# First q block on ScalarE's DMA queue, ahead of the activation table, with a new order of jobs

## The chip, the cores and the metric

The kernel runs on one core of a Trainium2 chip. Five engines work side by side: TensorE (PE in the profile; its weight loads are PEld), VectorE (DVE), ScalarE (ACT), GpSimd (POOL) and SyncE (SP), which here only issues DMAs. Each engine takes its own instructions in program order and waits on semaphores for the others. The metric is the device time of one execution in microseconds (us).

## The reference

Three layers in float32 (weights arrive as float64 bits):

1. Attention for q, k, v of shape 2 x 8 x 768 x 64. Each query sees the keys less than 16 positions away and, for each of 24 blocks of 32 keys, one summary: the maximum of the block's keys (score plus log 32) with the mean of its values. Softmax runs over both kinds of score at once.
2. A gated layer on x (2 x 768 x 512): `h = relu(x @ w_in)`, split into u and v; v is normalised per row, multiplied from the left by `w_spatial` (768 x 768), `b_spatial` is added, and `(u * v) @ w_out` is returned.
3. A convolution layer: `h = relu(x @ w_in)`, a three-tap convolution along the sequence, `(h * sigmoid(conv)) @ w_out`.

## The kernel before

Eight head pairs (2 batches x 4 pairs, n = 0 to 7) are worked on, each in two **groups** of six blocks of 64 queries, so 16 groups. A group is (`group`, line 447): scores on TensorE (`qk`: mask rows at L462 and L469, then 24 small matmuls of q against the scaled keys at L475); the negated row maximum on VectorE (L479); six exponentials with running sums on ScalarE (L483, twelve instructions); sum and reciprocal on VectorE (L486, L489); the scaling of the probabilities on GpSimd or VectorE (L492); two steps of three transposes on TensorE (L496), each copied out of PSUM (L518); 24 matmuls with the values (L502); and the split of the result in a high and a low part (L523, L524). The scores have two PSUM buffers, so group i + 2 waits until the exponentials of group i are done.

Before the groups of a pair, `keys` (line 379) scales the key windows (two halves, L388 or L390), takes block maxima over k (L398, two halves for the first four pairs) and places them scaled beside the windows (L404). `means` (line 409) makes the block means of the values: for pairs 0 and 2 with matmuls (L418), for the others with a reduction and a transpose (L425, L428), then copies them into place (L430, L437).

The weights arrive as float64 bits. `convert` (line 288) loads a part, builds the float32 with one product (L294 or L295) and three VectorE instructions (L297, L299, L301), and splits it in a high part (L285) and a low part (L279). Every dense product is then three matmuls (`mm3`, L310 to L312). The dense work of batch 0 is put between the attention steps of the later pairs as soon as its inputs exist; behind the attention only dense work is left.

What the engines do and in which order is set by two strings. Each piece of work is a job that is added with `add` (a dictionary of the engines that may do it with a cost in us, then what it reads and writes). `PICK` chooses the engine where there is a choice, and `ORDER`, two characters to a job, is the order in which the jobs are emitted, and so the program order on every engine and queue. `Plan.order` also keeps a clock of its own from the costs (jobs of the DMA queue are called "Q", and what they load counts as there `LAND` = 2.6 us after their cost). It uses that clock for one thing only: where a TensorE job ahead of the dense work would start at least 0.5 us after the previous one, it emits (gap - 0.1) / 0.22 filling matmuls on a constant tile (`warm`, L741). Seven warming matmuls of the same line start the program.

All DMAs are issued by SP's queue, in the order k (two parts), a part of w_in, the first half of q, k of the second pair, and so on. On ScalarE the first instruction is a dummy exponential (L736), which brings the load of the activation table with it.

Of the kernel before, what the change touches and what calls it, by code (L numbers as in the profile page):

```python
# [41 lines left out]
RATE = 276.0  # L42
# [13 lines left out]
    "EtDpEuC7C8C9C+C-BXEiDqDBCLFiEvFjE3E4EjEkDzD0EwFvCMCNDuDvCOCPD6DCDDDED7D8D9D1D+D2EEEFD3FBCQEGE5EmDFDGFkEHEIE6D4F6F7EOEPEQ"
    "ERGmD5F8F9C4FCD-EAEBECFWEXE7FFFGEYEZEaEbGnFHFIFJFKElFXEDE8GlEcEdE9FYFLGkFZFlFaGQGRGDE+ExEJEKELESHRGSGEGFEyFmE-FAFnEzFbFz"
    "F0EMFwGtG6GdEVJ8FQFRFcFdF1ENHHHIGeF2F3GfGGGgF4FeHSFSFTF5FoHJFUHTGhGiGjFpFqFrGuFDG7HUHVHKHLEWFsG8GTGUGHF+GVGIFtHMHNFuFfFg"
    "HlHmFxHnHoGJFyG9G+HOHWHbHcGvGKGwHdHXFhHpHYItGLGMF-GxGyGAHZH5GBHqIDH6HeGWGXIyGCH7FEGoH8HPHfHgGYHrHvGNGZGaGbHwHxHaGOGcGPHh"
    "G-H9H+HQGzG0HyGpGqLNIEG1G2GsGrH-IFIuHAHzH0HBIzINIOIPHCIIIvHsIAHiH1H2HtHuHDH3H4IBICIXIiI0HEG3IJIKHFLOLPHGILISI1G4G5HjI2Hk"  # L60
    "ITInIdIaIUIQIYIZIMLQIjIqJ5IVIWIkIlIGIRIoIpI6LRIHIbIcI3JHJIJJImIrIeJbLbI9I+JKIwJvI7IsJLJMI8JNJwI4I-JAIfJBJCJDJcI5JRJSIgJT"
    "JUJVJWJXJOJPJdJeJfJYJgJhJQJiIxKRJxJyKbJzJ0KHKIKJKKKLKlJjKmKMJkKNIhJEJFKSLULWJGKvJ9JlJmJnJoJpJqKwLDLEK5KOLSLTKPKQLVKcJ1Li"
    "J2JrJsK6KTK7J+J-LXKdKeLYJ3JtLdJ4KxLZKAKfKgJZLaLcLpKhJuKiKnKBKCKULFKVKjJaKkLeLGLHLfLkLgLhLjLwKDKyKzKWKXKYK0K1KZKEKFMrK8K9"
# [728 lines left out]

# [101 lines left out]
```

## Time and profile before

| | |
|---|---|
| runs before | 333.34 us median of 3 (331.83, 333.34, 337.34) |
| profiled execution | span 329.8 us from first to last instruction; its time with what lies around the span is not listed |
| busy, share of the span | PE 98%, PEld 82%, DVE 71%, ACT 57%, POOL 21% |
| granted TensorE clock, mean | 0.999 |
| DMA | 34.50 MB, mean 105 GB/s |

How to read it: a busy TensorE is not yet a useful one, since the filling matmuls count as busy. What an engine waits for stands behind "idle before" with the releaser. The chain of waits goes back from the last instruction, at each step to what released it. What matters for the start of the kernel lies in the first 40 us; all engines but GpSimd are close to full there, one after the other.

### The profile page before, as it was taken

How to read it: one execution, taken by the hardware profiler on the slowest of the kernel's cores; microseconds unless marked ns; L12 is line 12 of the kernel's file. 1: busy time of each engine (PE TensorE's matmuls, PEld its weight loads, DVE VectorE, ACT ScalarE, POOL GpSimd, SP SyncE). 2: the span in 40 equal slices, each digit the busy share in tenths (PEclk: the TensorE clock that was granted, in tenths of full speed). 3: DMA queues.
4: the chain of work that ended last, by engine and by line, in shares of the span. 5: the costliest groups of instructions: out<-in, count | busy, mean ns of one | idle time of the engine just before them, and what ended most of it. 6: DMA issues, size and time to landing. Idle time of an engine off the chain costs nothing.

```text
span 329.8 us, 6175 instructions
## 1 busy us (share of the span) xinstructions
PE 324.2 (98%) x2388; PEld 269.1 (82%) x2388; DVE 232.8 (71%) x435; ACT 189.6 (57%) x466; POOL 67.9 (21%) x86
## 2 busy tenths in 40 slices
PE   8999999999999999999999999999999999999996
PEld 3768888888888888888988888888888888888886
DVE  6989799877766456788989788689988776470000
ACT  3999889977357323534425355788857665461111
POOL 4695835641230131211001011200000000000000
PEclk9999999999999999999999999999999999999999
DMA  7999486905026600232334234400000010000101
GB/s 221 344 284 322 116 276 223 267 21 145 0 72 194 219 0 0 80 112 72 122 127 127 70 123 127 129 0 2 0 2 32 0 66 32 32 32 34 64 32 66
DMA packets 13325, 34.50 MB, mean 105 GB/s; under 512 B 1648, under 2 KB 3952, under 8 KB 13296
## 3 DMA queue, kind: packets, MB, share of 16 engines
q1 hardware_dynamic: 13296, 34.11, 33.5%
q8 instruction: 19, 0.31, 0.4%
q14 instruction: 10, 0.08, 0.1%
HBM read 30.96 MB, written 3.15 MB: 103 GB/s over the span
## 4 chain that ended last, share of the span: by engine, by line
PE 93%; ACT 2%; POOL 1%; DMA 1%; issue 0%; DVE 0%; SPq 0%; ACTq 0%; POOLq 0%
PE late L311 12%; PE late L310 12%; PE late L312 12%; PE mm L310 10%; PE mm L311 9%; PE mm L312 9%; PE pt L496 3%; PE xp L311 3%; PE xp L312 3%; PE xp L310 3%; PE pt L311 3%; PE xp L502 3%; PE pt L312 3%; PE pt L310 3%; PE s L475 2%; DMA a<-q_in 1%
## 5 line engine op out<-in xcount | busy, mean ns | idle before, releaser
L689 DVE SCALAR_TENSOR_TENSOR v<-v,conv_t 128x767 f32<-128x767 f32 x32 | 32.4, 1016 | 12.2 <-ACT v L686 11.8
L483 ACT ACTIVATE a<-s,a 128x120 f32<-128x120 f32 x96 | 33.4, 385 | 1.0 <-DVE a L479 0.9
L294 ACT ACTIVATE a<-a 128x512 f32<-128x512 f32 (+1 forms) x28 | 17.8, 636 | 16.4 <-DVE w L279 7.7
L299 DVE SCALAR_TENSOR_TENSOR a<-a,a 128x512 uint32<-128x512 uint32 (+1 forms) x32 | 19.9, 623 | 3.5 <-ACT a L294 1.7
L483 ACT ACTIVATION_READ_ACCUMULATOR a<-s,a 128x1 f32 x96 | 22.1, 231 | 0.0
L492 POOL TENSOR_TENSOR a<-a,a 128x720 f32<-128x720 f32 x14 | 19.7, 1419 | 5.5 <-DVE a L489 5.4
L301 DVE SCALAR_TENSOR_TENSOR a<-a,a 128x512 uint32<-128x512 uint32 (+1 forms) x32 | 20.0, 624 | 0.9
L310 PE MATMUL late<-xh,a 128*128 128x512 f32 x48 | 18.7, 389 | 0.0
L311 PE MATMUL late<-xl,a 128*128 128x512 f32 x48 | 18.7, 389 | 0.0
L312 PE MATMUL late<-xh,a 128*128 128x512 f32 x48 | 18.7, 389 | 0.0
L279 POOL TENSOR_TENSOR w<-a,w 128x256 fp32r<-128x256 f32 (+1 forms) x11 | 10.6, 969 | 38.8 <-ACT w L285 38.7
L692 ACT ACTIVATE v<-v 128x768 f32<-128x768 f32 x16 | 13.5, 843 | 8.4 <-DVE v L689 8.4
L570 POOL TENSOR_TENSOR stat<-stat,mhalf 128x1 f32<-128x1 f32 x12 | 9.1, 762 | 43.4 <-DVE stat L567 39.8
L496 PE MATMUL pt<-ident,a 128*120 128x128 f32 x96 | 16.5, 280 | 0.8 <-DVE a L518 0.6
L730 ACT COPY tmp<-late 128x512 f32<-128x512 f32 x7 | 4.1, 585 | 21.9 <-PE late L312 21.9
L695 DVE TENSOR_TENSOR v<-v 128x768 f32<-128x768 f32 x15 | 14.3, 954 | 3.1 <-ACT v L692 2.9
L565 DVE BATCH_NORM_STATS2 stat<-tmp 128x6 f32<-128x512 f32 x12 | 8.3, 691 | 11.4 <-ACT tmp L562 11.3
L285 ACT CAST w<-a 128x512 fp32r<-128x512 f32 (+1 forms) x15 | 8.3, 550 | 13.9 <-DVE a L301 13.9
L686 ACT ACTIVATE v<-v,conv_t 128x768 f32<-128x768 f32 x16 | 15.0, 938 | 1.8 <-DVE w L279 1.0
L496 PEld LDWEIGHTS pt<-ident,a 128*120 128x120 f32 x96 | 10.8, 137 | 5.3 <-POOL a L492 1.0
L518 ACT COPY a<-pt 120x384 f32<-120x384 f32 x21 | 10.3, 488 | 8.1 <-PE pt L496 7.9
L479 DVE TENSOR_REDUCE a<-s 128x6 f32<-128x720 f32 x16 | 14.2, 899 | 1.0 <-PE s L475 0.8
(336 smaller groups left out, 1033.0 us busy)
## 6 DMA issues: line engine op xcount, KB each, us to landing
a<-w_in SPq DMA_DIRECT2D x12, 512.0 KB, 3.6
a<-w_out SPq DMA_DIRECT2D x8, 512.0 KB, 3.6
out<-tmp SPq DMA_DIRECT2D x11, 256.0 KB, 2.0
a<-vwin SPq DMA_DIRECT2D x8, 288.0 KB, 6.1
a<-v_in SPq DMA_DIRECT2D x6, 384.0 KB, 6.0
a<-vwin SPq DMA_DIRECT2D x4, 576.0 KB, 5.9
tmp<-w_spT SPq DMA_DIRECT2D x6, 384.0 KB, 3.5
a<-w_in SPq DMA_DIRECT2D x8, 256.0 KB, 6.4
```

The costliest lines, as they stand in the source:

```text
L294: mul = {"ACT": (0.2 + n / 1080, lambda: ACT.mul(fu.f(), half(1).bitcast(F32), 2.0 ** -112)), "POOL": (0.18 + n / 1050, lambda: POOL.tenso ...
L299: add({"DVE": (0.16 + n / 960, lambda: DVE.scalar_tensor_tensor(out=last.u(), in0=fu.u(), scalar=0x80000000, in1=last.u(), op0=ALU.bitwise ...
L301: add({"DVE": (0.16 + n / 960, lambda: DVE.scalar_tensor_tensor(out=fu.u(), in0=fu.u(), scalar=3, in1=last.u(), op0=ALU.logical_shift_left ...
L310: PE.matmul(ps, lhsT=lh, rhs=rh, start=first and i == 0, stop=False)
L311: PE.matmul(ps, lhsT=lh, rhs=rl, start=False, stop=False)
L312: PE.matmul(ps, lhsT=ll, rhs=rh, start=False, stop=last and i == n - 1)
L483: ACT.activation(out=e[:, u, :NK], in_=sv[:, u // GA, u % GA], func=AF.Exp, bias=st[:, 0, u:u + 1], accum_out=sm[:, u, :1])
L492: eng.tensor_tensor(out=e, in0=e, in1=st[:, 1].unsqueeze(2).to_broadcast([128, GB, NK]), op=ALU.mult)
L496: PE.transpose(pt3[:NK, a], e[:, GA * h + a, :NK], ident)
L686: add({"ACT": (0.93, lambda: ACT.activation(out=ct.f(), in_=hh.f(), func=AF.Copy, scale=conv_t[:, 3 * f + 1:3 * f + 2]))}, r + 0.5, [hh.to ...
L689: DVE.scalar_tensor_tensor(out=ct.f()[:, to], in0=hh.f()[:, of], scalar=conv_t[:, 3 * f + k:3 * f + k + 1], in1=ct.f()[:, to], op0=ALU.mul ...
L695: eng.tensor_tensor(out=ct.f(), in0=hh.f(), in1=ct.f(), op=ALU.mult)
```

## The change

The load of the first half of q of the first head pair becomes a job of its own kind, "QA": `ACT.dma_start`, with a cost of 2.0 us in the planner. It is the first job of the new order. The dummy exponential becomes a job too (`table`) and comes fourth, so that on ScalarE the DMA issue stands ahead of the load of the activation table. The other loads stay on SP. Some planner costs change (the very first w_in part counts 165 KB more; the casts of `one_tile` count 0.6 us, with the table counted apart). `ORDER` and `PICK` are new from end to end.

```diff
 ORDER = (
-    "AAACABADAFAgAEAiAGAjAZAaAkAhAbAHAqAcAdAeArALBYAfAMBZBbBaBcAIA3A4AsAJAlAtASAUATAVAWAuAvANBiBjAKBEA5A6A7BFCTCRCUBkAmAnAwAx"
+    "AIABAGAAAHADACAFAiAaAjAkAlAEAcAMAhANAJAbBbBZArAsAOAdA4ATBcAeAKA5BdBaBFAPAUAtBjAmBGALAfB9AuAvAVAWBkA6AwCUAxA7BHA8BIAyBwB+"
...
-                t = max(t, end[j][0] + (self.LAND if end[j][1] == "Q" else 0.0 if end[j][1] == e else self.HAND))
+                t = max(t, end[j][0] + (self.LAND if end[j][1] in ("Q", "QA") else 0.0 if end[j][1] == e else self.HAND))
...
-        dma(0.8 * n, lambda: SP.dma_start(raw.u(), src.bitcast(U32)), rank - lead, writes=[raw.tok()])
+        dma(0.8 * n + (165 if rank - lead < 3 else 0), lambda: SP.dma_start(raw.u(), src.bitcast(U32)), rank - lead, writes=[raw.tok()])
...
-            dma((q1 - q0) / 2 * 0.84 + (166 if n + i == 0 else 0), lambda q0=q0, q1=q1: SP.dma_start(qts[j].ap[:, q0:q1], q_in[b, p][:, q0:q1]), r - 9 + 1.5 * i, writes=[qts[j].tok(q0, q1)])
+            on = {"Q": ((q1 - q0) / 2 * 0.84 / RATE, lambda q0=q0, q1=q1: SP.dma_start(qts[j].ap[:, q0:q1], q_in[b, p][:, q0:q1]))}
+            if n + i == 0:
+                on = {"QA": (2.0, lambda q0=q0, q1=q1: ACT.dma_start(qts[j].ap[:, q0:q1], q_in[b, p][:, q0:q1]))}
+            add(on, r - 9 + 1.5 * i - (100 if n + i == 0 else 0), writes=[qts[j].tok(q0, q1)])
...
-    ACT.activation(out=stat[0][:, 11:12], in_=mhalf, func=AF.Exp)
...
+    def table():
+        ACT.activation(out=stat[0][:, 11:12], in_=mhalf, func=AF.Exp)
+
+    add({"ACT": (2.2, table)}, -100, writes=[tok("table")])
...
-    add({"ACT": (2.65, one_tile)}, -99, [tok("ident")], [mask_b.tok(sub="o")])
+    add({"ACT": (0.6, one_tile)}, -99, [tok("ident"), tok("table")], [mask_b.tok(sub="o")])
```

The two strings, read two characters at a time and split by engine, begin like this (g0, g1 are a pair's two halves; w1b and w1a the second and first half of the first w_in tile; numbers of pairs and groups count from 0):

```
SP queue   before  k0a k0b w1b q0a | k1a k1b q0b vals0a w1a q1a vals0b k2a k2b q1b
           after   k0a k0b w1b     | k1a k1b q0b q1a w1a vals0a k2a q1b k2b vals0b     (q0a on ScalarE)
ScalarE    before  table casts scale(0,g1) w1b-high exp0 w1a-product exp1 scale(2,g0) exp2 mean copy w1a-high exp3 exp4 copy split copy exp5
           after   q0a table casts scale(0,g0) w1b-product scale(1,g1) exp0 exp1 exp2 copy scale(2,g1) exp3 copy split exp4 split copy scale(3,g1) exp5
VectorE    before  ... scale(0,g0) masks max k0a, k0b, place | w1b shift, or, or | max scores0 | max k1b, k1a | max scores1 | sum0 w1a x3 recip0
           after   ... masks max k0a, k0b, place | w1b shift | max k1a | max scores0 | w1b or | max k1b | w1b or | max scores1 | sum0 recip0
GpSimd     before  constants w1b-product scale(1,g0) w1b-low scale(1,g1) place1 normalise0 normalise1
           after   constants scale(0,g1) scale(1,g0) place1 w1a-product w1b-high normalise0 scale(2,g0) normalise1
TensorE    before  qk0 qk1 m0a qk2 m0b t0 qk3 t0 qk4 t1 pv0 t1 t2 qk5 pv1 t2 qk6 t3 m1 t3 dense qk7 pv2
           after   qk0 qk1 qk2 m0a t0 qk3 t0 m0b t1 qk4 t1 pv0 qk5 t2 pv1 qk6 t2 m1 m2a t3 qk7 pv2 dense
```

Here qk is the scores of a group, t one of its two transpose steps, pv its value product, m a pair's block-mean step. The planner's rule for filling matmuls, followed with each string and its costs, gives 6, 5 and 4 of them before (ahead of qk0, qk1 and the first t2) and 2, 3, 6 and 2 after (ahead of qk0, qk1, qk2 and qk6); the seven warming ones stay. In the whole string 88 jobs change their engine (GpSimd has 76 jobs before and 98 after, VectorE 391 and 375, ScalarE 286 and 281). The number of TensorE jobs stays at 515; its changes of tiling mode fall from 45 to 42. The last eight jobs of SP's queue stay as they are.

## Rows read from the trace of the kernel before

**Rows 1.** The page's first part: busy us (share of the span) and instructions of each engine.

```profile
PE 324.2 (98%) x2388; PEld 269.1 (82%) x2388; DVE 232.8 (71%) x435; ACT 189.6 (57%) x466; POOL 67.9 (21%) x86
```

**Rows 2.** Windows: stretch, its us, busy us of each engine, clock, DMA share, GB/s.

```profile
0.00:6.00 6.00, 4.96 (x21) 1.80 (x21) 3.27 (x25) 2.54 (x5) 1.97 (x12) 1.00 0.60 173
6.00:40.00 34.00, 32.53 (x591) 24.90 (x585) 29.85 (x70) 30.08 (x133) 26.37 (x33) 1.00 0.91 280
40.00:320.00 280.00, 280.00 (x1741) 236.06 (x1737) 199.71 (x343) 155.63 (x326) 39.53 (x42) 1.00 0.27 84
2.00:4.00 2.00, 2.00 (x7) 0.62 (x5) 0.98 (x8) 0.82 (x4) 0.60 (x3) 1.00 0.87 254
```

**Rows 3.** Windows of line L741 alone (PE and PEld busy, clock, DMA share, GB/s).

```profile
0.00:6.00 6.00, 4.87 (x13) 1.66 (x13) 1.00 0.60 173
6.00:40.00 34.00, 2.28 (x9) 0.80 (x9) 1.00 0.91 280
```

**Rows 4.** The chain of waits in order of time, 0 to 40 us: start, us, what.

```profile
2.08 4.27 DMA a<-q_in
6.49 0.88 PE s L475 x24
7.39 0.92 DVE a L479
8.33 2.17 ACT a L483 x12
...
24.67 0.12 PE mm L310
25.93 0.85 PE xp L502 x24
27.25 2.73 PE mm L418 x24
29.98 0.47 PE pt L496 x3
```

**Rows 5.** Timeline, 0 to 25 us: start, us, engine, line, operation [idle before <-releaser].

```profile
0.71 1.28 ACT L736 ACT_TABLE_LOAD   x1 [0.71 <-PEq L887]
0.72 0.85 SPq L363 DMA_DIRECT2D a<-k_in  x2
1.04 4.87 PE L741 MATMUL mm<-ones 128*128 128x512 bf16 x13 [1.04 <-DVE mhalf L735]
2.01 0.20 ACT L736 ACTIVATE stat<-mhalf 128x1 f32<-128x1 f32 x1
2.08 0.43 SPq L366 DMA_DIRECT2D a<-q_in  x1
2.12 0.49 ACT L767 CAST a<-ident 64x64 bf16<-64x64 f32 x2
3.21 0.46 DVE L390 TENSOR_SCALAR a<-a 128x576 f32<-128x576 f32 x1 [0.91 <-DMA a<-k_in]
3.76 0.68 ACT L388 ACTIVATE a<-a 128x576 f32<-128x576 f32 x1 [1.15 <-DMA a<-k_in]
4.39 0.54 DVE L398 TENSOR_REDUCE a<-a 128x12 f32<-128x384 f32 x1
4.97 0.31 DVE L404 TENSOR_SCALAR a<-a 128x288 f32<-128x288 f32 x1
5.76 0.29 DVE L297 TENSOR_SCALAR a<-a 128x256 uint32<-128x256 uint32 x1 [0.48 <-DMA a<-w_in]
6.97 0.81 POOL L390 TENSOR_SCALAR a<-a 128x576 f32<-128x576 f32 x1 [0.64 <-DMA a<-k_in]
8.21 1.00 DVE L398 TENSOR_REDUCE a<-a 128x12 f32<-128x384 f32 x2
24.13 0.54 PE L496 MATMUL pt<-ident,a 128*120 128x128 f32 x3 [0.61 <-DVE a L518]
```

**Rows 6.** Windows of all engines, from the first exponentials to the end of the sixth set.

```profile
8.30:24.60 16.30, 15.24 (x295) 11.45 (x295) 14.31 (x34) 15.70 (x80) 13.48 (x17) 1.00 1.01 315
```

More of the change, by code (lines that the diff above doesn't have):

```diff
@@ L56 @@
[L56 to L63, printed above, removed]
@@ L72 @@
-    "S0S1SZS2SsS3S4StS7S5SuS8S6TuS9SvS+SwTIS-TJTBTKTCTLTMTDTNTETOTPTFTSTQT7TTTGTRTUTHTVTfTWTgTYThTZTiTjTaTkTbTlTmTcTpTnTqTdTo"
-    "TrTeTsT2TtT3TvT4TwT5UDTxT6UET8UFTyT9UGUHTzUIT+T0UJT1UKT-UNULUAUOUMUPUBUQUCURUSUTUUUXUVUYUWUZUaUbUcUdUeUhUfUiUgUjUkUlUmUn"
-    "UoUrUpUsUqUtUuUvUwUxUyU1UzU2U0U3U4U5U6U7U8U-U9VAVBU+VCVDVEVFVGVJVHVKVIVLVMVNVOVPVQVRVS"
+    "AIABAGAAAHADACAFAiAaAjAkAlAEAcAMAhANAJAbBbBZArAsAOAdA4ATBcAeAKA5BdBaBFAPAUAtBjAmBGALAfB9AuAvAVAWBkA6AwCUAxA7BHA8BIAyBwB+"
+    "BLCSBlA9CVAzAnBxCWA0AXBmBnAoAQA+A-B-CTDICcByApBoDKBAA1DLAqCpARCdCEBBA2BzA3BpBNB0BeBJAYBMCqCeDMBCBDCAC2AZBOBEBqDSDJB1CFBr"
@@ new lines @@
+    "CfCgBsBfBKC3BgCrCXBPDTB2DfBiBhEfCsCtB3ASCuBtDxEUB4ChEhCYDUCLBuDgBSDVDWC4B5EiCiBvCZCjBQDhB6CGCkCHCIB7ClCaEgEoB8AgCvDiCwDX"
+    "CbCBCmFPEpCnCxCyBRCJE1CoDjDNEqCKBUDYCDEVCzDZBTFQC0C1DyErDsFNDaC6DODPDzDkEsDbDtCCJ6DlEjE2DRDQFCDcDdDeDmEtFODnC7C8DoDuC9EW"
+    "C+E3EuFwDpCMBVFWDqFjC-DBDADrBWEvBXFDDvCND0DwCOBYJ9D1EkEwE4E5D2D7FkEYF7DCD3FXE6D4CPD5DDFlElD8D6FGD9F8D+DEEADFExCQE7CREZD-"
+    "FRDGEBF9C5FYEFEGEaE8DHEHECE9GmFHEIEnEbEcEDFEF+EEF0FxGnFZE+FaFyEmGEGRFIGeGoGFEyFbGSEJFJE-EdFKEeEKFmGGELFLEPEQFAFnEzF1EREM"
@@ new lines @@
+    "ESFBENF2FMGlGTFcETGuEOF3GfG7HSHIE0F4GgFdFFGhFSF5FeF6GiHTFoEXGjHJHUFfHKGkFpG8HLFTGHFUGUFqHMHVFrHWFsGIFVF-HcGJFgHNFtGvFuFv"
+    "HmHdGwGKHOHPGLHnGpHoG9FzGMGVFhHeHfIuHgHpFiGWGNIjGXGAHXGYHqHQGxHwGBH6G+GZHxHYGCH7GyGDIkHZIEGaHaHrGbGOG-GzIzGPGcH8HyGdGQHz"
+    "G0HAIFHRIGG1HbH0G2H9HhI0IOG3GqH1HBIvH+GrHsHCHtIJGtH-H2LOGsIPIAHDHiH3IBIKG4HEHFIlG5HGH4IQG6ILHHLQIRHjH5I1I2HuITIMIULVIHIm"
+    "ICIIHvHkISIVIWIDIYIeIXI+INIfIZJIJJIwHlLPJSIoIgIaJcIbIpIhI-JdI3LRInJTJKJUIcIqIdJeIiJwIrIsJ7JLI4ItJVJMLSJmJAI7I5JNI6JnJWJx"
@@ new lines @@
+    "JBJXLcI8IxJOI9JCJfIyKIJPJDJgJyKmJEJhJQJzJoJiJRKcKdJ+J-JYJ8JFJZJpJGJHKAJ0J1KwKSKxJqLEJaKeK6K7KJJrLTLFKnLGLUJbJjLHLWKTJsLX"
+    "KBJ2KKK8KCJ3KLLYKMLZKDJ4KUJ5JkLaLbKfLjLeJtKNKyKgKEJlKoKFLdKpLfKOKVKPKhLgKWLILhLlKiLJJuKQLiKzKjNAMsLqK0LkK1LmLnKRKGK9K2Mt"
+    "JvMuKkK3LoKHKXKYKlLxLKNBKqK+LsM2KZKrKaLpK-MvK4MiLrM3MwKbLANeLtLuLBNfNoLLK5LvM4LwNULzLCLMNpLyMjNCM5L0KsNVKtNDL1L4NgLNNhNW"
+    "MkLDMxM6NiL2L3NKNEMlL6NLMmMyL5M7NXKuKvL-MnL7NFL8L9M8M9O2NqNGMoNMO3L+NNNjM+O8MzNOMBNYMAO4MCO9MDMENHMFMGMIM0NIMHMNMpNrMUM-"
@@ new lines @@
+    "MqNsO5NPMJMKO+MPOqNZMLMMO-MONkMQMROwOrM1MWOsMrO6MbMSOxNtMTOtNaNQPOPCNlMVPAPIMXOyMYOuNJNRPPPDO7NyMZNuPJMaOvMdPaNbPEMcOzPU"
+    "MePBO0PxPKMfN0MgPQPVMhO1PyPbNmPLPRNzPSPsPFN1NSN2NvN5PfPTN3PGOANnPcPdQQPMQRN7PeNTPzPgN4PhPHP0NcN6P2N8PtPiN9PjPuN+N-PvP+PW"
+    "PNQDP-OBOHPlOCQiPmPXPwODOEQEP1QAPYOFQ5QSQBQTPkP3QFQGOGQHQjNdP4QkPnOJNwPZQnP5Q6PoOIQVQWQCQXQJQoQYQ7OONxRGOKQ0PpQpP6PqOLOM"
+    "QIQKQlQ8Q1QUQZP7ONOQRYPrQqOPP8QbQLQcQmQ2RZQsRLRMORRNQ3P9OSQrOVQMQdRaQtOTOXOUR3OWQNOYRbQaQeROQ4Q9RqQuQvSERHQ+RdSFRrQOReQw"
@@ new lines @@
+    "RIRJRsSOQfQPQxSGOjQgQ-OZSPOcQhOaQyOeObRQRKOdRPRfRASbRRScRBRSR4OfRgSlOgSmRiRtRTRCRhQzRcOhR5OiSySzRURDRvRjSdSeSQSHS0SfRuRE"
+    "SnS1OlS8RkRFRVOkSgS2OmOnSRRlRwOoR8RmS9RWSIRnOpR6SoTJR7RXRxTKRoTLRpSJRySTS3ShSKTMSSR9SLRzR0SMSUSVR1TqTTSWTUR+TNSXSqTOS+TV"
+    "TgTWSpR-SASiSYTYSjSBTrR2S-SCTPTXS4TQTsTBSDT3ThTASZSrUEUFUYTCTiTRSaTDTjSsTkStTETZSuTlS5UiSvUZUjS6TtSkTFUOUGTuTmTaTnUaVATv"
+    "UkTbT4SwUsUPT5UHUISxTGTHTwTcTIUtTxUuT6SNTyT8UJT7TzVBTdT0UQTeToUbURUcUlT9UvUSTfT1U2VCT2UmT+T-VKUTS7UAUwVDUBUnUCUxVLUKUdUD"
@@ L75 @@
+    "ULUeUUU3UMVEUoTpU4UpUVUyUfVFVMVNTSUqUWVOUzUNU5U6U7UgU8UXU9UhVGUrU0VPU1U+VHVQU-VIVRVSVJVT"
 )
 PICK = (
-    "001101210000101011001110100010000010100011000100011010100010111010000100010001010101001100011111011000011000100000000001"
-    "110000011001010110010000000000000011010000010100100001000000000000000200200000000200200200200"
+    "111011101000100010011110101010100100101111011010111010000011110010100100011000110100010100010100010110120001110001001000"
+    "120111111000111011000011000001100011000100110011001010000011100100010101100011011100001201201"
```

11 lines of the change are left out of this document (removed).

## The prediction

> **What bounds it now.** I read the busy times first, then the windows by stage, then the chain of waits, then the timeline of the first 14 us. TensorE is busy for 98% of the span [rows 1]. The windows say where the other 2% lies: from 40 to 320 us it is busy 280.00 of 280.00 us, and up to 40 us it is idle for 1.04 us (before 6) and 1.47 us (34.00 - 32.53) [rows 2]. The rest of its idle time is the tail, in which the last block is copied and stored; the change leaves that tail as it is. But busy is not useful: 7.15 us are the warming and filling matmuls of L741, 4.87 of them before 6 us and 2.28 behind that [rows 3]. The number of real matmuls is fixed. So the end of the kernel is set by how much of the first 40 us TensorE spends on nothing: 2.51 us idle and 7.15 us filling, 9.7 us in all, and that is the most that any change of the head could touch.
>
> The chain shows what holds the head: the first q block (issued at 2.08, landed at 6.35), the first scores (6.49), their maximum on VectorE (7.39), their exponentials on ScalarE (8.33) [rows 4]. From there to 24.6 us ScalarE is busy 15.70 of 16.30 us and VectorE 14.31 [rows 6]: in that stretch they set the pace and TensorE follows. After it TensorE has dense work to fill every gap.
>
> **The q block.** It leaves SP's queue, where it was fourth and issued at 2.08 us, and leaves ScalarE's queue first. SP's first issue started at 0.72 us, and ScalarE's table load at 0.71, so I put the new issue at 0.7. The first k block took from 0.72 to 3.21 us, when VectorE, which had waited for it, started [rows 5]. With the two running side by side I take 3.2 to 3.7 us for q, against 6.35: it arrives about 2.9 us sooner.
>
> **What is late next.** The first scores also need the scaled keys. In the kernel before, the last step of those ended at 4.97 + 0.31 = 5.28 us [rows 5]. In the new order VectorE no longer scales the first half (0.46 us; ScalarE does it in 0.68), but the two maxima over k still take 0.54 us each and the second needs the second k block, landed by 3.76. If k is not delayed at all, this ends at 3.76 + 0.54 + 0.31 = 4.6 us; if q's 192 KB take their full time out of 254 GB/s (0.76 us), at 5.4. TensorE itself is occupied by the 7 warming matmuls and, by the planner's rule with the new costs, 2 fillers instead of 6. Started at 1.04 [rows 5], 9 of the 13 end at 4.4 at the mean of 4.87 / 13; if the last 4 ran at the 0.25 us that the later ones take (2.28 / 9), the first 9 end at 4.9 [rows 3]. I take 5.2 for the first q product, 1.3 us sooner than 6.49.
>
> **Why little of that arrives.** The chain then goes through VectorE, and there the new order puts two jobs ahead of the first maximum that wait for transfers: the shift of the first w_in part and the maximum of the second head pair's first k block. In the kernel before, w_in landed by 5.76 and that k block by 6.97 [rows 5]. Counted in bytes, q's block was queued ahead of this k block before and still is, so the k block cannot come much sooner: 7.0, or 6.5 if the second queue fills what is unused (the DMA engines were 87% busy in 2 to 4 us [rows 2]). So the first maximum of scores starts at 7.0 to 7.5 after the 0.50 us reduction: I take 7.4, as before (7.39).
>
> A page of the Trainium skill speaks against the move: "DMA: Bandwidth & Descriptors", section "Issuing engines are not separate DMA queues", says that transfers issued by different engines run on the same 16 DMA engines and interleave, so that a second issuer saves only issue time. By that rule only the issue (1.36 us) is gained, q lands at 5.0, k and w_in pay, and the first maximum starts at 7.5; without it, at 7.0. No run before shows two load queues at once.
>
> **ScalarE.** Its DMA issue (0.43 us, SP's row) now stands ahead of the table load (1.28), the dummy exponential (0.20) and the two casts (0.49) [rows 5]. All shift by 0.43, the casts end at 2.12 + 0.49 + 0.43 = 3.0 us, and the first user of them is after 4.4: this costs nothing while the warming matmuls cover it. Then ScalarE must do two jobs ahead of the first exponentials: the w_in product, free at about 6.3 + 0.4, and the scaling of the second pair's second half, which waits for the second k block (landed at the latest at 8.21 [rows 5]; my value 7.6, for its 192 KB behind the first) and takes 0.68. So exponentials start at about 8.3, as before (8.33). Bounds: 7.9 and 8.9.
>
> From there to the end of the sixth set the old order had 8 other jobs on ScalarE: 15.70 - 6 x 2.1 = 3.1 us, or 0.39 each. The new one has 7: three copies, two casts and two scalings, 5 x 0.39 + 2 x 0.68 = 3.3 us. The old stretch had 0.60 us idle; the new one begins with three sets in a row, and I give it 0.25. The sixth set ends at 8.3 + 12.6 + 3.3 + 0.25 = 24.45 instead of 24.6.
>
> **TensorE's side.** Here the new order does help. In both orders the scores of the eighth group and then a value product (0.85) follow that set. The scores took from 25.03 (the dense step before them, three matmuls from 24.67 at 0.12) to 25.93, 0.90 us. So the new order has the value product done at 24.45 + 0.90 + 0.85 = 26.2, against 25.93 + 0.85 = 26.78 before [rows 4]: 0.58 us. By that point it has done one block-mean product more (half of the two at 2.73: 1.37), one transpose step less (0.47), and not yet the dense step of 0.36 that the old one had slipped in: 1.37 - 0.47 - 0.36 = 0.54 us more useful work. **Sum:** 0.58 + 0.54 = 1.1 us. Fillers fall from 15 to 13 with the same covers, and the changes of tiling mode from 45 to 42; both are inside that sum. On SP's queue all that stood behind q moves up by one issue (0.43 us), but the first values go behind the second pair's q and the other part of w_in, 448 KB or 1.6 us at 280 GB/s [rows 2]. Their user, the first block means, now stands behind the third scores, which wait for the first exponentials (8.3 + 2.1) anyway; without that cover it would cost up to 1.6 us, against which only the fillers ahead of those scores stand. Behind 26 us I cost the new order at nothing: TensorE has dense work waiting. If that cover is gone in places, each hole is priced like the longest wait on TensorE between 6 and 40 us, 0.61 us [rows 5].
>
> The span would be 329.8 - 1.1 = 328.7 us. The profiled execution lies 2.0 us under the fastest run shown and 3.5 us under the median; taking the 1.1 off the median gives **332.2 us**. The bounds of the start of the exponentials (0.4 better, 0.6 worse) and 0.5 us for the walk to 26 us make this case 331.3 to 333.3.
>
> **Rivals.** *Nothing arrives* (0.13): q was on the chain only because nothing else was late, and the ScalarE stretch of 16.3 us keeps its length and its TensorE work. For it: 15.70 of 16.30 busy. Against: the work counted above. 333.3 us.
>
> *Slower through ScalarE's queue* (0.15): its first exponentials stand behind two jobs that wait for transfers. If the second pair's second k block lands after 7.7 us, every 0.1 us later is 0.1 us on the whole stretch, which has no slack. At 8.7 us the exponentials start at 9.4, 1.1 later; less the 0.54 us of better packing that is 333.9. For it: the upper bound of 8.21 on that landing. Against: as many bytes stand ahead of it as before.
>
> *Holes behind 26 us* (0.09): the old order has none from 40 to 320 us, so a new one can only equal it or lose. Three holes of 0.61 less the gain: 334.1.
>
> *The packing is much better* (0.08): the 2.28 us of fillers and 1.47 us of waits between 6 and 40 us vanish by three quarters, 2.8 us: 330.5. For it: that waste is there. Against: it covers waits for ScalarE and VectorE, which have as much to do as before.
>
> *The table is still first* (0.05): if the load of the table is placed ahead of the issue, q leaves at 2.0 us, which is where the next instruction began after it [rows 5], and lands between 4.5 and 6.3; since the scores' maximum waits for k anyway, 332.2 to 333.3. The Trainium skill ("ScalarE: Activation LUTs", "What ACT_TABLE_LOAD costs") adds a drain of about 1.38 us to the 1.28 of the load, which would put the issue at 3.4 and the time at the upper end; the trace has the 1.28 but no such gap behind it, and the row decides.
>
> **Chances.** The forecast has 0.50. The cases lie within 330.5 and 334.1, and runs of one kernel here differ by more (331.83 to 337.34), so that a change under 2% (6.7 us) can't be told from none. The range for 8 in 10 is 329.5 to 335.0: all cases, with about 1 us for the median of a few runs. Faster by over 2% would need two thirds of the head's 9.7 us and has 0.03; slower by over 2% would need eleven holes and has 0.04; 0.93 lies between.
>
> **What would show it.** Right: an ACT-queue transfer of q issued at 0.7 and landed before 4; first q product at 4.9 to 5.5; 20 matmuls on L741; the first score maximum still at 7.0 to 7.5 behind a reduction of k; the first exponentials at 7.9 to 8.9; TensorE busy without a break from 40 us on. Wrong: the table load ahead of the issue; k or w_in later than 4.3 and 6.5; idle TensorE behind 30 us; or the sixth set of exponentials over a microsecond away from 24.5.

## The result, and the profile after

The changed kernel takes 335.09 us (median of 10 runs, 333.54 to 336.72); the kernel before, run beside it, 332.72 us (median of 10, 331.83 to 337.34). The ratio is 1.0071 with a 95% interval of [1.0046, 1.0096]: 2.4 us slower where 1.1 us faster was forecast, and just above the range's upper end of 335.0. The profiled execution has a span of 334.0 us (329.8 before) and took 335.8 us. One thing is needed to read the runs: in five of the ten the mean granted clock is 0.993 to 0.995, as in the profiled one, and in the other five it is 1.0; the first five average 335.6 us, the others 334.6.

The page's first part and the windows of the changed kernel, in the columns of [rows 1] and [rows 2]:

```profile
PE 326.2 (98%) x2386; PEld 269.8 (81%) x2386; DVE 242.4 (73%) x419; ACT 185.2 (55%) x460; POOL 107.2 (32%) x108
```

```profile
0.00:6.00 6.00, 4.90 (x33) 1.84 (x37) 2.94 (x23) 2.54 (x5) 2.52 (x12) 1.00 0.67 196
6.00:40.00 34.00, 30.30 (x548) 22.56 (x542) 30.10 (x62) 28.97 (x128) 25.71 (x33) 0.95 0.94 287
24.00:40.00 16.00, 13.69 (x237) 10.87 (x236) 13.92 (x26) 13.64 (x57) 12.55 (x17) 0.89 0.94 285
40.00:320.00 280.00, 280.00 (x1761) 236.00 (x1756) 209.35 (x334) 150.02 (x321) 78.96 (x63) 1.00 0.25 78
```

From 40 us on nothing has changed for TensorE: 280.00 of 280.00 us. GpSimd is busy 107.2 us instead of 67.9 and VectorE 242.4 instead of 232.8, and behind 40 us that costs TensorE nothing. The loss lies ahead of 40 us: TensorE is idle there for 1.10 + 3.70 = 4.80 us against 2.51, and between 24 and 40 us it was granted 0.89 of its clock. The 20 filling matmuls (L742 now) take 4.02 us before 6 and 2.90 behind it, 6.92 us against 7.15 [rows 3].

The timeline of the changed kernel, 0 to 14 us (start, us, engine, line, operation, idle before and its releaser), against [rows 5]:

```profile
0.71 0.40 ACTq L368 DMA_DIRECT2D a<-q_in  x1
...
3.93 1.08 DVE L401 TENSOR_REDUCE a<-a 128x12 f32<-128x384 f32 x2 [0.73 <-DMA a<-k_in]
...
5.56 0.85 PE L478 MATMUL s<-a,a 64*64 64x120 f32 x24
...
6.44 0.29 DVE L297 TENSOR_SCALAR a<-a 128x256 uint32<-128x256 uint32 x1 [0.98 <-DMA a<-w_in]
...
6.97 0.55 DVE L401 TENSOR_REDUCE a<-a 128x12 f32<-128x384 f32 x1 [0.23 <-DMA a<-k_in]
...
7.44 0.90 DVE L482 TENSOR_REDUCE a<-s 128x6 f32<-128x720 f32 x1
...
8.37 0.36 ACT L486 ACTIVATE a<-s,a 128x120 f32<-128x120 f32 x1 [0.20 <-DVE a L482]
...
11.11 1.39 POOL L495 TENSOR_TENSOR a<-a,a 128x720 f32<-128x720 f32 x1 [0.63 <-DVE a L492]
11.23 1.54 DVE L299 SCALAR_TENSOR_TENSOR a<-a,a 128x256 uint32<-128x256 uint32 x1
...
13.63 0.36 ACT L486 ACTIVATE a<-s,a 128x120 f32<-128x120 f32 x1 [1.04 <-DVE a L482]
```

Up to the first exponentials (8.37) the forecast holds. Then comes a row that it does not have: a step of the w_in conversion that takes 0.42 us elsewhere takes 1.54 at 11.23, beside a GpSimd multiplication. The maximum of the next scores stands behind it on VectorE, and ScalarE waits 1.04 us for that maximum at 13.63.

The same thing happens again at 31 us, with a larger effect. First VectorE, then GpSimd, then TensorE of the changed kernel, cut out of 28 to 40 us:

```profile
30.72 0.82 DVE L297 TENSOR_SCALAR a<-a 128x256 uint32<-128x256 uint32 x1
31.65 1.42 DVE L299 SCALAR_TENSOR_TENSOR a<-a,a 128x256 uint32<-128x256 uint32 x1
33.10 0.83 DVE L301 SCALAR_TENSOR_TENSOR a<-a,a 128x256 uint32<-128x256 uint32 x1
33.86 0.54 DVE L526 CAST xh<-xp 128x384 fp32r<-128x384 f32 x1
34.43 0.56 DVE L527 TENSOR_TENSOR xl<-xp,xh 128x384 fp32r<-128x384 f32 x1
```

```profile
30.66 0.73 POOL L279 TENSOR_TENSOR w<-a,w 128x256 fp32r<-128x256 f32 x1
31.35 1.44 POOL L495 TENSOR_TENSOR a<-a,a 128x720 f32<-128x720 f32 x1
32.75 0.90 POOL L279 TENSOR_TENSOR w<-a,w 128x256 fp32r<-128x256 f32 x1
```

```profile
31.57 0.79 PE L478 MATMUL s<-a,a 64*64 64x120 f32 x24
...
35.14 0.92 PE L505 MATMUL xp<-a,a 120*64 120x64 f32 x24 [2.31 <-DVE a L489]
...
36.84 1.41 PE L478 MATMUL s<-a,a 64*64 64x120 f32 x24
```

Lay the ends side by side. The three VectorE steps end at 31.54, 33.07 and 33.93; the three GpSimd instructions end at 31.39, 32.79 and 33.65, each 0.15 to 0.28 us before "its" VectorE step. In the same place of the kernel before, the same steps were free and GpSimd stood idle:

```profile
30.21 0.29 DVE L297 TENSOR_SCALAR a<-a 128x256 uint32<-128x256 uint32 x1
30.42 0.42 DVE L299 SCALAR_TENSOR_TENSOR a<-a,a 128x256 uint32<-128x256 uint32 x1
30.88 0.42 DVE L301 SCALAR_TENSOR_TENSOR a<-a,a 128x256 uint32<-128x256 uint32 x1
```

```profile
32.16 0.40 POOL L285 CAST w<-a 128x256 fp32r<-128x256 f32 x1 [3.11 <-DVE a L301]
```

Behind the three steps stand L526 and L527, which split a value product and so empty the PSUM bank that the next value product needs. TensorE waits 2.31 us for them. (The row names the small reduction L489 as releaser, as the last event to come; it takes 0.15 us.) After that wait the matmuls run at the lower of the two clock levels for a while: the granted clock of a window from 37 to 39 us is 0.50 (1.2 GHz), and the same 24 score matmuls take 1.41 us instead of 0.79.

One row for each kernel sums it up, that of L299 ahead of 40 us (instructions of its one shape, 128x256: duration in ns, min/median/max; first and last start). Before, then after:

```profile
L299 DVE SCALAR_TENSOR_TENSOR a<-a,a x5: 410/419/426, 6.4 to 31.2; 128x256 uint32<-128x256 uint32 x5
```

```profile
L299 DVE SCALAR_TENSOR_TENSOR a<-a,a x4: 416/920/1545, 8.3 to 31.6; 128x256 uint32<-128x256 uint32 x4
```

In the kernel before not one of the five is held: its order keeps GpSimd and these steps apart, so this row shows a price of 0.42 us and nothing else. Its trace is not free of holds, though. GpSimd's scaling at 6.97 takes 0.81 us [rows 5] beside an or (6.82 to 7.24), where the same scaling takes 0.67 alone; one of the two shifts at 28.71 takes 0.48 instead of 0.28 beside another scaling; and a multiplication at 85.89 takes 1.72 instead of 1.39. Counting every instruction that takes over 0.1 us more than is usual for its form, I find 2 on VectorE and 5 on GpSimd in the whole kernel before, 1.4 us in all, and 28 and 24 in the changed one, 21 and 7 us. Only those of the first 40 us meet work that TensorE waits for.

**The sum.** Idle TensorE 4.80 - 2.51 = 2.29 us, fillers -0.23, and about 1.5 us for the lower clock level, found by taking each operation from 35.99 to 39.00 against the same one earlier (0.08 + 0.04 + 0.14 + 0.62 + 0.35 + 0.26): 3.6 of the 4.2 us between the two spans. The rest I can't place; the ends of matmuls are modelled. Counted in matmuls that have ended by 40 us (prices in the part on the gain below), the changed kernel is 3.9 us behind, an estimate.

### The profile page after: what moved, and what is told of

Read it like the earlier page. It is cut to its first block, busy times and chain, and to the rows that moved or that the text cites. A ratio compares the mean times of both kernels' runs of the same rounds, so it can differ in the third digit from the quotient of the medians.

```text
span 334.0 us, 6198 instructions
## 1 busy us (share of the span) xinstructions
PE 326.2 (98%) x2386; PEld 269.8 (81%) x2386; DVE 242.4 (73%) x419; ACT 185.2 (55%) x460; POOL 107.2 (32%) x108
## 4 chain that ended last, share of the span: by engine, by line
PE 93%; DVE 3%; DMA 1%; ACT 1%; SPq 0%; issue 0%; DVEq 0%
PE late L310 12%; PE late L311 12%; PE late L312 12%; PE mm L310 10%; PE mm L311 9%; PE mm L312 9%; PE pt L499 3%; PE xp L311 3%; PE xp L310 3%; PE xp L312 3%; PE xp L505 3%; PE pt L311 3%; PE pt L310 3%; PE pt L312 3%; PE s L478 2%; DMA a<-k_in 1%
## 5 line engine op out<-in xcount | busy, mean ns | idle before, releaser
L692 DVE SCALAR_TENSOR_TENSOR v<-v,conv_t 128x767 f32<-128x767 f32 x32 | 37.5, 1184 | 13.3 <-ACT v L689 6.5
L299 DVE SCALAR_TENSOR_TENSOR a<-a,a 128x512 uint32<-128x512 uint32 (+1 forms) x32 | 23.6, 737 | 5.6 <-ACT a L294 4.8
L279 POOL TENSOR_TENSOR w<-a,w 128x256 fp32r<-128x256 f32 (+1 forms) x13 | 12.9, 992 | 45.5 <-ACT w L285 41.5
L698 POOL TENSOR_TENSOR v<-v 128x768 f32<-128x768 f32 x5 | 11.8, 2351 | 40.9 <-ACT v L695 40.9
L294 ACT ACTIVATE a<-a 128x512 f32<-128x512 f32 (+1 forms) x25 | 16.2, 647 | 13.0 <-POOL w L279 2.9
L301 DVE SCALAR_TENSOR_TENSOR a<-a,a 128x512 uint32<-128x512 uint32 (+1 forms) x32 | 22.3, 696 | 0.7
L495 POOL TENSOR_TENSOR a<-a,a 128x720 f32<-128x720 f32 x13 | 18.6, 1433 | 4.5 <-DVE a L492 3.1
L698 DVE TENSOR_TENSOR v<-v 128x768 f32<-128x768 f32 x11 | 11.8, 1074 | 8.1 <-ACT v L695 8.1
L297 DVE TENSOR_SCALAR a<-a 128x512 uint32<-128x512 uint32 (+1 forms) x32 | 14.2, 443 | 1.2 <-DMA a<-w_in 1.0
L573 POOL TENSOR_TENSOR stat<-stat,mhalf 128x1 f32<-128x1 f32 x12 | 7.8, 669 | 22.1 <-DVE stat L570 22.1
L279 POOL TENSOR_TENSOR a<-a,a 128x512 fp32r<-128x512 f32 x4 | 6.4, 1595 | 26.2 <-ACT a L285 26.2
```

The costliest lines, as they stand in the source:

```text
L279: eng.tensor_tensor(out=lo.r(), in0=src.f(), in1=hi.f(), op=ALU.subtract)
L294: mul = {"ACT": (0.2 + n / 1080, lambda: ACT.mul(fu.f(), half(1).bitcast(F32), 2.0 ** -112)), "POOL": (0.18 + n / 1050, lambda: POOL.tenso ...
L299: add({"DVE": (0.16 + n / 960, lambda: DVE.scalar_tensor_tensor(out=last.u(), in0=fu.u(), scalar=0x80000000, in1=last.u(), op0=ALU.bitwise ...
L301: add({"DVE": (0.16 + n / 960, lambda: DVE.scalar_tensor_tensor(out=fu.u(), in0=fu.u(), scalar=3, in1=last.u(), op0=ALU.logical_shift_left ...
L495: eng.tensor_tensor(out=e, in0=e, in1=st[:, 1].unsqueeze(2).to_broadcast([128, GB, NK]), op=ALU.mult)
L692: DVE.scalar_tensor_tensor(out=ct.f()[:, to], in0=hh.f()[:, of], scalar=conv_t[:, 3 * f + k:3 * f + k + 1], in1=ct.f()[:, to], op0=ALU.mul ...
```

## The experiments

The theory after the comparison: VectorE's conversion steps are held while GpSimd works beside them; in the new order that happens at two places that other engines wait for, and the q block on the second queue has little to do with it. The rivals: q on ScalarE's queue does harm through the transfers that it delays; the split of L526 is simply too far back in VectorE's order, with or without GpSimd; and both orders are held back by the first score maximum, so that an earlier one would beat them. Each run below is a change of a few lines. Where jobs are moved, they are moved in the list that `Plan.order` reads from `ORDER`, with this helper:

```diff
+        def ahead(jobs, of):
+            for k in jobs:
+                seq.remove(k)
+                seq.insert(seq.index(of), k)
```

### q_alone: the old order, only q and the table moved

```diff
         seq = [64 * SIGNS.index(ORDER[i]) + SIGNS.index(ORDER[i + 1]) for i in range(0, len(ORDER), 2)]
+        seq = [8, 0] + [k + 1 for k in seq if k != 7]
```

`ORDER` and `PICK` are those of the kernel before; everything else is the changed kernel's.

> The old order and engine choices with q's first block on ScalarE's queue and the table behind it; nothing else moved. Theory A (the new order is to blame: VectorE's weight conversion is held beside GpSimd and keeps TensorE waiting at 32.8 us): the loss is not here; 331.8 to 333.0 us, ratio 0.997 to 1.001, no TensorE wait over 0.7 us behind 10 us, clock 1.00 in 24 to 40 us. Theory B (q on a second queue delays the other loads and that costs): 334 to 335.5 us, ratio 1.004 to 1.009.

Measured: 333.0 us (12 runs) against 332.67, ratio 1.0004 [0.9979, 1.0029]. Moving q by itself is worth nothing. The chain of waits of this kernel shows what is late next (start, us, what):

```profile
1.62 4.71 DMA a<-w_in
...
7.42 0.57 DVE a L302
...
8.12 0.91 DVE a L483
```

The first scores are there by 7.3, but in the old order the first maximum (8.12) stands behind three conversion steps that wait for w_in. The third of them is itself held: L302 takes 0.77 us at 7.42, where others take 0.42, beside a GpSimd scaling from 7.21 to 7.92. So in the old order, too, an early q meets this effect, for 0.35 us. Nothing else broke: from 6 to 40 us the clock is 1.00, and no wait on TensorE is over 1.28 us.

### order_alone: the new order, q back on SP's queue

```diff
+        ahead([8], 12)
+        ahead([0], seq[0])
...
-                on = {"QA": (2.0, lambda q0=q0, q1=q1: ACT.dma_start(qts[j].ap[:, q0:q1], q_in[b, p][:, q0:q1]))}
+                on = {"QA": (2.0, lambda q0=q0, q1=q1: SP.dma_start(qts[j].ap[:, q0:q1], q_in[b, p][:, q0:q1]))}
```

> The new order with q's first block back on SP's queue, behind the first w_in part, and the table first. Theory A: as slow as the changed kernel or a little slower, 334.5 to 336 us, with the 2.3 us wait of TensorE near 33 us again. Theory B: the loss goes, 332.5 to 333 us.

Measured: 336.03 us (7 runs), ratio 1.0099 [1.0064, 1.0134]. The new order loses without the second queue as well. TensorE's two long waits, and the held step of the first place:

```profile
7.27 0.85 PE L486 MATMUL s<-a,a 64*64 64x120 f32 x24 [2.06 <-DMA a<-q_in]
...
36.36 0.92 PE L513 MATMUL xp<-a,a 120*64 120x64 f32 x24 [1.83 <-DVE a L497]
```

```profile
12.70 1.55 DVE L307 SCALAR_TENSOR_TENSOR a<-a,a 128x256 uint32<-128x256 uint32 x1
```

The hole near 35 us is there again, with 1.83 us. But part of this loss is the run's own: the wait of 2.06 us for the late q, behind which the granted clock is 0.53 from 8 to 10 us, while behind the hole at 36 us it stays 1.00. So it is q_alone, not this run, that clears the second queue. The point estimates make the second queue worth 0.9 us inside the new order (336.03 - 335.09), which has only two fillers left to cover a late q; the two intervals overlap, so this is a hint and not a finding.

### split_first: the split ahead of the three conversion steps

```diff
+        ahead([123, 124], 134)
```

> The changed kernel with one edit of the order: the split of group 3 (two VectorE jobs) is put ahead of the three conversion jobs of a w_in part that stand in front of it. Theory A: the value product at 35.14 us starts 2 us sooner, TensorE's wait there falls from 2.31 us to under 0.5, the clock stays at 1.00 behind it; 331.5 to 333.0 us. Theory B: no change from 335.1. Theory C (22 more jobs on GpSimd hold VectorE all over, no single place): under half of the loss comes back, 334 us or more.

Measured: 333.91 us (12 runs), ratio 1.0029 [1.0009, 1.0049]: half of the loss is back, by the medians, less than theory A had expected. The value product that had waited 2.31 us (TensorE of this kernel):

```profile
30.89 0.92 PE L512 MATMUL xp<-a,a 120*64 120x64 f32 x24 [0.19 <-DMA a<-vwin]
```

All 12 runs have a mean clock of 0.999 or 1.0. The steps themselves are still held (0.75 and 0.77 us for the first two), but this product waits for them no more; at 37.26 TensorE waits 0.70 us for a later split, which stands behind them on VectorE. That the hole came from these steps is shown; that GpSimd is what lengthens them is not yet.

### held_probe: the disputed step by itself

The kernel before with a probe behind its last product: twelve GpSimd multiplications of 128x720, beside them twice a round of five VectorE instructions on other memory, and the same two rounds again when GpSimd is done.

```diff
+        for _ in range(12):
+            POOL.tensor_tensor(out=b[:, 0:720], in0=b[:, 0:720], in1=b[:, 720:1440], op=ALU.mult)
+        dve_ops()     # twice: shift L865, or L866, maximum L867, copy out of PSUM L868, three-operand step L869
+        DVE.tensor_copy(a[:, 1430:1431], b[:, 0:1])     # waits for GpSimd
+        dve_ops()
```

> The kernel before with a probe behind its end, on scratch data: ten VectorE operations of five kinds while GpSimd runs twelve multiplications of 128x720, then the same ten alone. Its total time is not of interest. Theory A: the shift and the or of the conversion (both operands in SBUF) take up to 1.4 us beside GpSimd and 0.3 to 0.45 alone, a reduction or a copy from PSUM the same in both. Theories B and C in a form without holding: all kinds within 10% in both.

Measured, VectorE of the probe (the second round beside GpSimd, then the second round alone), and GpSimd (its line, duration in ns, min/median/max):

```profile
307.54 1.83 DVE L865 TENSOR_SCALAR v<-v 128x256 uint32<-128x256 uint32 x1
309.41 1.91 DVE L866 SCALAR_TENSOR_TENSOR v<-v 128x256 uint32<-128x256 uint32 x1
311.24 0.54 DVE L867 TENSOR_REDUCE v<-v 128x12 f32<-128x384 f32 x1
311.70 0.54 DVE L868 COPY v<-xp 120x384 f32<-120x384 f32 x1
312.17 1.57 DVE L869 SCALAR_TENSOR_TENSOR v<-v,conv_t 128x767 f32<-128x767 f32 x1
...
328.86 0.29 DVE L865 TENSOR_SCALAR v<-v 128x256 uint32<-128x256 uint32 x1
329.19 0.42 DVE L866 SCALAR_TENSOR_TENSOR v<-v 128x256 uint32<-128x256 uint32 x1
...
330.45 1.01 DVE L869 SCALAR_TENSOR_TENSOR v<-v,conv_t 128x767 f32<-128x767 f32 x1
```

```profile
L860 POOL TENSOR_TENSOR v<-v x12: 1735/1742/2342, 303.2 to 324.5; 128x720 f32<-128x720 f32 x12
```

The shift goes from 0.29 to 1.83 us, the or from 0.42 to 1.91, the 767 wide step from 1.01 to 1.57. The maximum (0.54) and the copy out of PSUM (0.54) are not touched: alone they take 0.54 and 0.55. GpSimd pays too: a multiplication of this probe takes 1.74 us alone, as the last six of the twelve do, and two of them, which started at 306.88 and 313.00 behind a 767 wide step that VectorE had begun, take 2.34. So the hold is an effect of the pair of engines, not of that place in the kernel.

### pool_later: VectorE's order untouched, two GpSimd jobs moved back

```diff
+        ahead([32, 81], 83)
```

The two low-part jobs (L279 in the changed kernel) now stand behind the three conversion steps.

> The changed kernel with two GpSimd jobs (low parts of two w_in halves, which nothing needs yet) moved from beside the three held VectorE steps at 30.7 to 33.9 us to behind them; VectorE's own order is untouched. Theory A (VectorE is held by what GpSimd runs beside it): the three steps take 1.5 to 2.2 us together instead of 3.1 (1.1 if nothing ran beside them; the probabilities' scaling, 1.4 us, still does), TensorE's wait falls from 2.31 to 1.0 to 1.6 us, 333.6 to 334.5 us. Theory G (the three steps are long for another reason, and the order on VectorE alone matters): no change, 334.7 to 335.5 us.

Measured: 333.87 us (12 runs) against 332.68, ratio 1.0034 [1.0009, 1.0058]. VectorE's steps and TensorE's wait of this kernel:

```profile
30.08 0.35 DVE L304 TENSOR_SCALAR a<-a 128x256 uint32<-128x256 uint32 x1
30.53 1.42 DVE L306 SCALAR_TENSOR_TENSOR a<-a,a 128x256 uint32<-128x256 uint32 x1
31.98 0.42 DVE L308 SCALAR_TENSOR_TENSOR a<-a,a 128x256 uint32<-128x256 uint32 x1
```

```profile
33.61 0.92 PE L512 MATMUL xp<-a,a 120*64 120x64 f32 x24 [1.42 <-ACT a L445]
```

The two steps whose GpSimd neighbour went away fell from 0.82 and 0.83 to 0.35 and 0.42 us; the middle one, which still has the 128x720 multiplication beside it (30.25 to 31.67), stays at 1.42. TensorE's wait fell by 0.89 us, about what the two steps gave back (0.47 + 0.41). (The split now ends at 33.47, and the last 0.1 us of the wait belongs to ScalarE's copy, which ends at 33.56.) So the place of the split was not the whole cause: nothing on VectorE was moved here. The clock of all 12 runs is 0.999 or 1.0 here, with a wait of 1.42 us left. Behind 40 us TensorE waits once more, 0.89 us at 48.30 for ScalarE's scaling of keys (L398).

### split_max_first and max_no_fill: the first hold as well

On top of split_first, the maximum of the second scores is put ahead of the step that was held at 11.23. The planner's rule then emits 5 fillers more ahead of the first transposes; the second of the two kernels leaves these out.

```diff
+        ahead([100], 22)          # both
...
-                    n = int((gap - 0.1) / 0.22)
+                    n = int((gap - 0.1) / 0.22) * (k != 49)          # max_no_fill alone
```

> As split_first, and the maximum of group 2's scores is put ahead of the VectorE conversion step (L299) that was held for 1.54 us at 11.2 us in the changed kernel. Theory A (held steps ahead of chain work): the third set of exponentials starts at 12.7 to 13.0 us instead of 13.63, and another 0.3 to 1.0 us comes back: 332.9 to 333.6 us, ratio 1.000 to 1.002. Theory F (what is left of the loss lies in ScalarE's and VectorE's amount of work up to 40 us): as split_first, 333.6 to 334.1 us, ratio 1.003.

Measured: 334.31 us (12 runs) against 332.73, ratio 1.0049 [1.0026, 1.0072], no better than split_first and slower than theory A expected.

> As split_max_first, without the 5 filling matmuls that its order brought ahead of the first transpose step. Theory A: third set of exponentials 0.5 to 1 us sooner than in split_first relative to the second; 332.8 to 333.5 us, ratio 1.000 to 1.002. Theory F (what is left lies in the amount of work): 333.6 to 334.1 us, ratio 1.003.

Measured: 333.17 us (12 runs) against 332.68, ratio 1.0016 [0.9999, 1.0033]. The two differ by five fillers, and by 1.1 us: 5 x 0.22 by the planner's own price, and 1.25 us in the trace of split_max_first (at 15.73). The two intervals overlap a little, so the size is rough. In max_no_fill the transposes behind that place start without a wait: a filler ahead of work that is ready costs its length, whatever gap the planner expected there. In max_no_fill the third set of exponentials no longer waits for its maximum. Against split_first it gains 0.7 us by the medians, but the two intervals overlap. The traces are clearer: from the first exponentials to the end of the sixth set the changed kernel takes 17.10 us, split_first 17.10 and pool_later 17.12; max_no_fill and all_three, without this hold, take 16.55 both. So the hold costs this stretch 0.55 us of the 1.04.

### all_three: both, and the GpSimd jobs moved back

max_no_fill with `ahead([32, 81], 83)`.

> max_no_fill and pool_later in one kernel. Theory A: the best of the new order, 332.3 to 333.3 us, ratio 0.999 to 1.002. Theory F: 333.4 us or more.

Measured: 333.12 us (12 runs) against 332.68, ratio 1.001 [0.9994, 1.0025]. VectorE's steps in the place of the hole, and its window from 6 to 40 us:

```profile
31.56 0.32 DVE L306 TENSOR_SCALAR a<-a 128x256 uint32<-128x256 uint32 x1
31.99 0.42 DVE L308 SCALAR_TENSOR_TENSOR a<-a,a 128x256 uint32<-128x256 uint32 x1
32.45 0.42 DVE L310 SCALAR_TENSOR_TENSOR a<-a,a 128x256 uint32<-128x256 uint32 x1
```

```profile
6.00:40.00 34.00, 33.07 (x586) 24.69 (x580) 29.83 (x69) 30.82 (x131) 26.83 (x35) 1.00 0.98 290
```

Three steps in 1.16 us instead of 3.07, TensorE idle for 0.93 us between 6 and 40 instead of 3.70, clock 1.00. With the holds at these two places gone the loss is 0.4 us, which can't be told from nothing.

### new_lead and old_lead: is the first maximum worth more?

Both pull the first score maximum, and what it needs, ahead of VectorE's jobs that wait for transfers: new_lead on top of the new order with the split and the second maximum moved, old_lead on top of q_alone. The fillers ahead of the first scores are held at 2, others at 6.

```diff
+        ahead([9], 26)                             # both
+        ahead([33, 43, 44, 56, 57], 28)            # new_lead; old_lead without 33
+        ahead([45], 27)                            # new_lead; old_lead ahead of 31
...
+                    n = min(n, 2 if k == 43 else 6)
```

> As split_max_first, and the early q is made use of: the second half of q goes ahead of the first w_in part on SP's queue, the first two score maxima go ahead of the conversion on VectorE and of the maximum over the next pair's k, the first exponentials ahead of the w_in product on ScalarE, and no gap gets more than 6 filling matmuls. Theory D (the early q bought nothing because the first maximum waited for w_in and for the next k block): first exponentials at 7.0 to 7.4 us instead of 8.37, 1 us off: 331.9 to 332.8 us, ratio 0.997 to 1.000. Theory F: the exponentials start sooner and the time stays, 333.4 us or more.

> As q_alone (old order, q on ScalarE's queue), with the same edits for the early q: second half of q ahead of w_in, two score maxima ahead of the conversion, first exponentials ahead of the copy of the high part, 2 fillers ahead of the first scores and at most 6 elsewhere. Theory D: first exponentials at 7.0 to 7.4 us, 0.7 to 1.2 us faster than the kernel before: 331.5 to 332.0 us, ratio 0.996 to 0.998. Theory F: 332.4 to 333.2 us, ratio 0.999 to 1.002.

Measured: new_lead 336.14 us (6 runs), ratio 1.0088 [1.0058, 1.0119]; old_lead 335.97 us (8 runs), ratio 1.0101 [1.0068, 1.0134]; the kernel before 332.73. The hope failed. The first exponentials begin at 7.81 and 8.21 us, against 8.37 in the changed kernel and 9.05 in q_alone, and the time is lost again at once. (These are single traces. The six kernels that start with the changed kernel's orders up to there begin their exponentials anywhere from 7.53 to 9.04, so that most of this gain could be chance.) TensorE of new_lead:

```profile
5.33 1.48 PE L490 MATMUL s<-a,a 64*64 64x120 f32 x24
...
11.89 0.85 PE L490 MATMUL s<-a,a 64*64 64x120 f32 x24 [1.52 <-POOL a L419]
```

The first scores, begun 0.23 us earlier than in the changed kernel and behind as many fillers, take 1.48 us instead of 0.85: their matmuls take 0.40 to 0.46 us each, those of the changed kernel 0.26 to 0.32. The profile lists a granted clock of 1.00 for both, so why is not shown. The third scores then wait 1.52 us for GpSimd's L419, whose input VectorE now makes later. In old_lead TensorE waits 1.44 us at 9.40 for the values, and 0.43 in q_alone. So the start does not hang on the first maximum alone.

## Why the prediction was wrong

**q's issue and landing: right, a little fast.** The issue started at 0.71 as forecast (0.7). From issue to landing took 3.4 us, so it landed at 4.1 instead of 3.2 to 3.7, still 2.2 us sooner than 6.35. In the five other traces with the same start it landed at 3.7 to 4.0.

**What the other transfers pay: right in kind.** The first k block is used at 3.93 instead of 3.21 [rows 5], w_in at 6.44 instead of 5.76; the second pair's k block at 6.97 as before. For k this holds in every trace: it lands at 3.5 to 3.9 in the six kernels with the new start, and at 3.2 and 3.3 in the two with the old one (the kernel before, and held_probe, which is the same kernel up to its end). For w_in it does not: 5.1 to 6.9 in the six, 5.7 and 6.2 in the two, so its 0.7 us may be chance. The Trainium skill ("DMA: Bandwidth & Descriptors", "Issuing engines are not separate DMA queues") says that such transfers interleave on the same 16 engines; these rows agree in kind; the landing at 5.0 that I worked out by it was 0.9 us too late.

**The head up to the first exponentials: right, with some luck.** First q product 5.56 (5.2 forecast, bounds 4.9 to 5.5; 5.3 to 5.5 in the other five traces), first maximum 7.44 (7.4) behind a reduction of k, first exponentials 8.37 (8.3), table load behind the issue, 20 matmuls on L742, TensorE full from 40 us. The luck is in the transfers: in the six traces with this start the second pair's k block, which the first maximum stands behind, lands at 6.1 to 7.6 us, and the first exponentials begin at 7.5 to 9.0. The kernel before has 8.33, and 8.81 in held_probe. A forecast from one trace can't be better than that.

**The ScalarE stretch: wrong by 1.0 us, and this is the first half of the failure.** The sixth set ends at 25.47 instead of 24.45. The forecast gave ScalarE 15.9 us of work and 0.25 us of idle time; measured are 15.67 and 1.43 (8.37 to 25.47), 1.04 of it at 13.63. The cause is a VectorE step of 0.42 us that took 1.54. I walked VectorE with durations from the kernel before, in which none of the two-operand steps is held. max_no_fill and all_three, which take this hold off ScalarE's path, shorten the stretch from 17.10 to 16.55 us. The other 0.4 us over the forecast's 16.15 are not this hold's. A wait of 0.38 us for a value product, at 19.54, stands in all three traces.

**"Behind 26 us I cost the new order at nothing": wrong, and the second half.** The step priced each hole at 0.61 us and expected none. One came, of 2.31 us, from the same cause three times in a row: 3.07 us for steps that take 1.16. It also brought the lower clock level for a stretch, about 1.5 us in the profile and 1.0 us between the runs with a mean clock of 0.993 to 0.995 and the others. (For runs without a trace it is not known where the clock fell. The kernel before has such a mean in 3 of its 72 executions beside the experiments, with 335.3 to 335.8 us, so this hole is not the only thing that brings it.) Of the 48 runs of the four kernels that shorten or remove this hole without adding a filler ahead of ready work (split_first, pool_later, max_no_fill, all_three) none shows it. Removing the hole gives 1.2 us by the medians (split_first).

**The gain of 0.58 + 0.54 us: not seen at the end.** The fillers fell as forecast (20 matmuls), but the walk to 26 us rested on a sixth set that came 1.0 us late. all_three, in which both holds are off the path, is the test. Its sixth set ends at 24.84, its value product at 26.72 against 26.78: of the 0.58 there is 0.06. At that moment it has ended 12 block-mean matmuls more than the kernel before, 3 transposes less and 3 dense ones less, just what the forecast listed, 0.54 us at its prices. By 40 us that is gone. Both have then ended 240 score matmuls, 45 transposes, 48 of block means and 15 dense ones (9 of them narrow in all_three, 6 before), and 149 and 144 of values: at the prices of the kernel before (24 scores 0.61, 24 of values 0.85, 3 transposes 0.47, 12 of block means 1.37, a dense one 0.12 or 0.23) all_three is 0.2 us behind, an estimate. Its busy time up to 40 us less the fillers is longer (38.03 - 6.92 = 31.11 against 37.49 - 7.15 = 30.34), since the same score matmuls took longer; the longest set, where others take 0.79:

```profile
31.03 1.25 PE L487 MATMUL s<-a,a 64*64 64x120 f32 x24
```

Behind 40 us it waits once more, for 0.34 us at 46.72. With the 0.2 that is about the 0.44 us by which it ends later (333.12 against 332.68); the two traced spans differ by 1.0 us, and the rest of that I can't place. So the step "Behind 26 us I cost the new order at nothing" failed here too: the 0.54 us were won by 26 us and lost again by 40.

**The rivals.** "Holes behind 26 us" had 0.09 and was the right one in kind: one hole with its clock instead of three of 0.61. What the forecast could have read: the new order gives GpSimd 98 jobs instead of 76, the code marks these jobs of VectorE and GpSimd as `lock` and its planner never lets two of them overlap in its own clock (the chip does not follow that clock), and the old order's conversion steps lie where GpSimd is idle (3.11 us of it up to 32.16, released by L301). The trace of before had the effect only in small (0.81 us for a scaling at 6.97 [rows 5], 0.67 elsewhere), and no long hold on VectorE; but with 22 more jobs on GpSimd the new order asked for a bound, for example one GpSimd instruction of 1.39 us for each step that meets one. The Trainium skill has the rule as well ("SBUF — State Buffer", "Who interferes with whom"): a VectorE instruction with two SBUF inputs contends with a GpSimd instruction that reads SBUF, and the port pair that they share is an exclusive lock. The probe agrees for the or (0.42 to 1.91) and for the reduction, which the page says never contends (0.54 and 0.54). For the shift, with one SBUF input, the page has contention only in VectorE's two-port modes; it was held (0.29 to 1.83), and though no trace names the mode, 256 more elements cost a shift of the kernel before 0.13 us (0.29 to 0.42) and an or 0.27 (0.42 to 0.69), so that the shift handles about two in the time of one.

**The base.** The forecast started from 333.34, the median of three runs; ten runs give 332.72. That is 0.6 us of the 2.9 between forecast and result in the other direction, so the change itself was missed by 3.5 us.
